# Batch 1's attention earlier and its x transposed by DMA, with the loads of batches 2 and 3 held until those transposes have landed

## The chip, the cores and the metric

The kernel runs on one core of a Trainium2 chip. The metric is device time in microseconds (us), the median of several executions. The span of a profile (from the first to the last instruction) is about 2 us shorter than the time of the same run. A run is called slow when it lies over 1.5% above the fastest run of the same kernel; such runs are left out of the ratios, but not out of the medians quoted. In the profile's lines PE is TensorE (PEld its loading of weights), ACT ScalarE, DVE VectorE, POOL GpSimd and SPq the queue of SyncE. PSUM is the memory into which TensorE's products go; a PSUM pair is two of its buffers.

## The reference

Linear attention on 8 batches of 8 heads, 576 rows and 64 columns, then two matrix products with a SiLU between them on the 4608 x 512 result.

```python
phi = lambda x: np.where(x > 0, x, np.exp(x) - 1.0) + 1.0
q_p, k_p = phi(q), phi(k)
kv  = np.einsum('bhsd,bhse->bhde', k_p, v)
z   = np.sum(k_p, axis=2)
num = np.einsum('bhsd,bhde->bhse', q_p, kv)
den = np.einsum('bhsd,bhd->bhs', q_p, z)[..., None] + 1e-06
x = (num / den).transpose(0, 2, 1, 3).reshape(4608, 512)
h = x @ w_in                                  # 512 -> 2048
g = h * (1.0 / (1.0 + np.exp(-beta * h)))
out = g @ w_out                               # 2048 -> 512
```

## The kernel before

The kernel is a pipeline over batches. While TensorE computes batch b's first product (H, four x tiles of 128 rows against w_in) and its second (Y, against w_out), the attention of batch b+1 is put between the matmuls, from a `plan` that says after which group of matmuls what is issued. In the text, H2 is the first product of batch 2 and Y1 the second product of batch 1. A batch has four x tiles of 128 rows and a tail of 64; two batches' tails are done together at the end.

The scheduling that the change touches, cut:

```python
load_w_out(2); load_v(1); load_w_out(3)        # the queue of loads during H0
...
load_next(2)                                   # k, q, v of batch 2
h_last(0, xT[0], [])
...                                            # batch 1: exponentials, relu, phi, v copy
y_phase_wide(0, {
    4: [F(load_next, 3)],                      # k, q, v of batch 3
    10: [F(q_trans, 1, 0, 1, 2, 3), F(kv_mm, 1), F(kv_evac, 1), F(w_out_scale, 3, 2)],
    11: [F(num_mm, 1, 0), F(num_norm, 1, 0)],
    12: [F(num_mm, 1, 1), F(num_norm, 1, 1), F(x_trans, 1, 0, wide=True)],
    13: [F(num_mm, 1, 2), F(num_norm, 1, 2), F(x_trans, 1, 1, wide=True)],
    14: [F(num_mm, 1, 3), F(num_norm, 1, 3), F(q_trans, 1, 4)],
})
h_phase(1, ...)                                # x_trans(1, 2), x_trans(1, 3), load_v(4) in it
h_last(1, xT[1], [F(exp_, 2, 0), F(exp_, 2, 1)])   # 16 matmuls, exponentials, 4 SiLUs
exp_(3, 1); exp_(3, 0); silu_table()
y_phase_wide(1, {
    1: [F(phi, 2, 0), F(q_trans_dma, 2), F(phi, 2, 1)],
    6: [F(kv_mm, 2), F(kv_evac, 2)],
    8: [F(num_mm, 2, 0), F(num_norm, 2, 0)],   # 9, 10, 11: tiles 1, 2, 3
    ...
})
```

`kv_mm` is the product of keys and values. `num_mm` multiplies one tile of q_pT, the transposed phi(q), with it; `num_norm` divides on VectorE and gives x, which `x_trans` transposes (into xT) on TensorE or, from batch 2 on, one DMA per tile. `q_trans_dma` transposes all of phi(q) of a batch by one DMA. Loads are issued by GpSimd and cast fp32 to bf16; transposes by DMA and stores are issued by SyncE. A load is held back so: GpSimd first copies one element of the tile that must be there.

```python
def hold(a):
    nc.gpsimd.tensor_copy(held, a)

def held_v(b, n):                              # v of b behind q_pT of n
    if b < B:
        hold(st[n, "qT"][0:1, NJ, KC - 1, 0:1])
        load_v(b)
```

## Time and profile before

| | before |
|---|---|
| time, median of 3 (range) | 292.67 us (292.13 to 292.94) |
| span of the profiled run | 290.1 us |
| TensorE busy | 281.8 us, 97% |
| H1, Y1 start | 51.56, 66.44 us |
| batch 2: key-value product, first product with q_pT | 72.57, 75.06 us |
| H2 starts | 82.04 us |

Positions are us from the start of the span.

The granted clock, one digit for each of 40 equal slices of the span in tenths of full speed (the 7 is at the start-up):

```profile
PEclk9799999999999999999999999999999999999999
```

### The profile page before, as it was taken

What the parts mean: (1) busy time and instruction counts of PE and PEld (TensorE: products, weight loads), DVE (VectorE), ACT (ScalarE), POOL (GpSimd) and SP (SyncE); (2) the same over time, 40 slices, a digit from 0 to 9 for tenths busy, and PEclk for the clock granted to TensorE, in tenths of its full rate; (3) what the DMA queues carried; (4) which work ended last, traced back from release to release, by engine and by line L of the source; (5) the groups of instructions that cost most, each with busy time, mean ns of one, the idle gap of its engine ahead of it and who ended that gap; (6) DMA issues with size and microseconds to landing.
All of it is one profiled execution on the core that took longest, in us unless ns stands there. A gap on an engine that the chain in (4) does not pass through costs nothing.

```text
span 290.1 us, 4739 instructions
## 1 busy us (share of the span) xinstructions
PE 281.8 (97%) x1895; PEld 144.1 (50%) x1895; DVE 116.7 (40%) x235; ACT 174.0 (60%) x232; POOL 54.3 (19%) x79
## 2 busy tenths in 40 slices
PE   8889999999999999999999999999999999999994
PEld 3567445644576444454444444554455444444443
DVE  3784487504670365326532654163517300110021
ACT  2788798889998843875277617771750086018500
POOL 8924564400051205020402040000000000000000
PEclk9799999999999999999999999999999999999999
DMA  8999999999379956977894879433503500120033
GB/s 143 196 206 345 254 281 194 257 167 158 62 208 180 136 140 106 196 103 162 121 211 53 161 92 197 77 103 107 97 2 90 111 36 0 72 76 0 0 74 73
DMA packets 75766, 38.07 MB, mean 131 GB/s; under 512 B 43344, under 2 KB 70240, under 8 KB 75744
## 3 DMA queue, kind: packets, MB, share of 16 engines
q0 software_dynamic: 38912, 20.19, 49.0%
q1 hardware_dynamic: 36640, 17.44, 25.7%
q8 instruction: 15, 0.25, 0.4%
q10 hardware_dynamic: 192, 0.14, 0.2%
q14 instruction: 7, 0.06, 0.1%
HBM read 36.71 MB, written 9.44 MB: 159 GB/s over the span
## 4 chain that ended last, share of the span: by engine, by line
PE 92%; DMA 3%; POOL 3%; ACT 1%; issue 0%; DVE 0%; POOLq 0%
PE mm L527 42%; PE mm L475 41%; PE att L421 3%; DMA w_in<-in_moe_w_in_dram 3%; PE att L475 2%; PE att L362 2%; POOL xqk L135 1%; PE mm L559 1%; POOL vraw L135 1%; ACT q_pT L387 1%; PE mm L455 0%; PE att L395 0%; PE att L455 0%; DVE xT L385 0%; DVE y_sb L385 0%
## 5 line engine op out<-in xcount | busy, mean ns | idle before, releaser
L467 ACT ACTIVATE g<-mm,beta_c 128x512 bf16<-128x512 f32 (+2 forms) x160 | 97.8, 623 | 87.1 <-PE mm L475 87.0
L527 PE MATMUL mm<-w_out,g 128*128 128x512 bf16 x560 | 128.0, 379 | 0.0
L475 PE MATMUL mm<-xT,w_in 128*128 128x512 bf16 (+2 forms) x576 | 107.6, 344 | 1.3 <-DMA w_in<-in_moe_w_in_dram 1.2
L475 PEld LDWEIGHTS <-w_in 128*128 128x128 bf16 x672 | 63.8, 98 | 60.8 <-DMA w_in<-in_moe_w_in_dram 1.3
L527 PEld LDWEIGHTS <-g 128*128 128x128 bf16 x560 | 53.1, 98 | 59.0 <-issue 0.3
L537 DVE COPY y_sb<-mm 128x512 f32<-128x512 f32 x27 | 18.7, 692 | 72.9 <-PE mm L527 69.4
L229 ACT ACTIVATE e<-xqk 128x2560 bf16<-128x2560 bf16 x14 | 31.9, 2328 | 0.1
L242 DVE TENSOR_TENSOR qk_p<-r,e 128x2560 bf16<-128x2560 bf16 x14 | 20.8, 1491 | 12.8 <-ACT e L229 12.1
L437 DVE TENSOR_TENSOR xs<-att,rden 128x512 bf16<-128x512 f32 x36 | 24.9, 691 | 1.2
L372 DVE CAST kv_bd<-att 64x260 bf16<-64x260 f32 x14 | 6.0, 427 | 36.6 <-PE att L362 36.5
L435 DVE TENSOR_SCALAR den<-att 128x8 f32<-128x8 f32 x36 | 5.9, 163 | 26.8 <-PE att L421 26.8
L421 PEld LDWEIGHTS <-q_pT 128*128 128x128 bf16 (+1 forms) x160 | 11.1, 102 | 9.5 <-issue 1.3
L421 PE MATMUL att<-kv_bd,q_pT 128*128 128x130 bf16 (+1 forms) x160 | 14.8, 226 | 0.4 <-ACT q_pT L387 0.3
L475 PE MATMUL mm<-xT_tail,w_in 128*128 128x512 bf16 x64 | 14.0, 379 | 0.0
L595 POOL COPY held<-xT 1x1 bf16<-1x1 bf16 x4 | 2.0, 509 | 63.6 <-DMA xT<-xs 63.6
L237 DVE TENSOR_SCALAR r<-xqk 128x2560 bf16<-128x2560 bf16 x14 | 11.9, 853 | 4.0 <-DMA xqk<-in_q_dram 2.5
L612 PE MATMUL mm<-g 128*128 128x512 bf16 x30 | 9.3, 464 | 1.2 <-DVE g L145 1.2
L229 ACT ACT_TABLE_LOAD x7 | 9.0, 1283 | 0.1
L72 POOL DMA_DIRECT2D vraw<-in_v_dram x7 | 6.4, 909 | 10.1 <-DVE vaug L385 4.2
L72 POOL DMA_DIRECT2D xqk<-in_q_dram x7 | 7.1, 1021 | 3.9 <-ACT w_out L214 2.1
L436 DVE RECIPROCAL rden<-den 128x8 f32<-128x8 f32 x36 | 7.3, 203 | 1.2
L72 POOL DMA_DIRECT2D xqk<-in_k_dram x7 | 6.5, 935 | 5.3 <-DMA w_in<-in_moe_w_in_dram 2.5
(77 smaller groups left out, 138.1 us busy)
## 6 DMA issues: line engine op xcount, KB each, us to landing
out_dram<-y_sb SPq DMA_DIRECT2D x28, 256.0 KB, 2.4
xqk<-in_k_dram POOLq DMA_DIRECT2D x7, 512.0 KB, 9.0
xqk<-in_q_dram POOLq DMA_DIRECT2D x7, 512.0 KB, 10.7
vraw<-in_v_dram POOLq DMA_DIRECT2D x7, 512.0 KB, 12.2
w_in<-in_moe_w_in_dram POOLq DMA_DIRECT2D x4, 512.0 KB, 10.1
g<-in_moe_w_out_dram POOLq DMA_DIRECT2D x4, 512.0 KB, 10.9
out_dram<-y_sb SPq DMA_DIRECT2D x14, 128.0 KB, 5.2
xqk<-in_moe_w_out_dram POOLq DMA_DIRECT2D x2, 512.0 KB, 13.7
```

The costliest lines, as they stand in the source:

```text
L72: eng.dma_start(out=dst[:, :, 0:NJ, :].rearrange("p h j d -> p h (j d)"), in_=src[b, :, 0:MAIN, :].rearrange("h (p j) d -> p h (j d)", j=NJ),)
L229: nc.scalar.activation(st[b, "e", a][:, h0:h1], xqk[b % NX][:, a, h0:h1], ACTF.Exp)
L237: nc.vector.tensor_scalar(st[b, "r", a][:, h0:h1], xqk[b % NX][:, a, h0:h1], 0.0, 1.0, ALU.max, ALU.add)
L242: nc.vector.tensor_tensor(st[b, "p"][:, a].rearrange("p j (h d) -> p h j d", h=H)[:, h0:h1], st[b, "r", a][:, h0:h1], st[b, "e", a][:, h0: ...
L421: nc.tensor.matmul(nps[r0 : r0 + n, p // 2, c0 : c0 + 2 * (D + 1)], st[bb, "qT"][:, t, p, :n], kv_bd[bb % 2][:, p], start=True, stop=True, ...
L436: nc.vector.reciprocal(rden[:n], den[:n])
L437: nc.vector.tensor_mul(xs[:n], nv[:, :, :, 0:D], rden[:n, :, :, None].to_broadcast([n, 2, 4, D]))
L467: nc.scalar.activation(g_sb[b % 2][:, ff, c0:c1], hp[:, c0:c1], ACTF.Silu, scale=beta_c[:, ff : ff + 1],)
L475: nc.tensor.matmul(hp[:, c0:c1], w_in_sb[ff // 4][:, kc, (ff % 4) * P : (ff % 4 + 1) * P], x[:, t0:t1, kc, :] if b < B else x[:, kc, c0:c1 ...
L527: nc.tensor.matmul(yp, g_sb[b % 2][:, ff, t * P : (t + 1) * P], w_out_sb[ff // 4][:, ff % 4, :], start=(ff == 0), stop=(ff == FC - 1),)
L537: nc.vector.tensor_copy(y_sb, yp)
L612: nc.tensor.matmul(st["warm"], g_sb[0][:, FC - 1, 0:P], g_sb[0][:, FC - 1, :], start=True, stop=True, skip_group_check=True,)
```

## The change

The intent: bring batch 1's attention forward by two groups of Y0 (with v of batch 1 loaded earlier for it), so that x is ready early enough to be transposed by DMA, which takes 16 transposes off TensorE; and to keep the queue free for these DMAs, load batches 2 and 3 only behind them.

```diff
-    def by_dma(b):
-        return b >= DMA_T
+    def by_dma(b, t):
+        return b > 0 or t == NJ
...
-    load_w_out(2)
     load_v(1)
+    load_w_out(2)
     load_w_out(3)
...
-    load_next(2)
     h_last(0, xT[0], [])
...
     y_phase_wide(0, {
-        4: [F(load_next, 3)],
-        10: [F(q_trans, 1, 0, 1, 2, 3), F(kv_mm, 1), F(kv_evac, 1), F(w_out_scale, 3, 2)],
-        11: [F(num_mm, 1, 0), F(num_norm, 1, 0)],
-        12: [..., F(x_trans, 1, 0, wide=True)],
-        13: [..., F(x_trans, 1, 1, wide=True)],
+        7: [F(kv_mm, 1), F(w_out_scale, 2, (0, 1), False), F(q_trans, 1, 0, 1, 2, 3),
+            F(kv_evac, 1), F(w_out_scale, 2, (2, 3))],
+        9: [F(num_mm, 1, 0), F(num_norm, 1, 0), F(w_out_scale, 3, range(4), False)],
+        10: ...                                  # num_mm and num_norm of tiles 1, 2, 3
     })
+    def load_late():
+        hold(xT[1][0:1, NJ - 1, KC - 1, 0:1])    # the fourth x tile of batch 1
+        for b in (2, 3):
+            load_k(b)
+            load_q(b)
+            if b == 2:
+                load_v(b)
     h_phase(1, xT[1],
-        [(ff, 0, 2) for ff in range(4)] + [(ff, 2, 4) for ff in range(4)] + ALL[4:12],
+        [(ff, 0, 2) for ff in range(8)] + [(ff, 2, 4) for ff in range(8)] + ALL[8:12],
-            0: [F(x_trans, 1, 2), ...], 1: [F(x_trans, 1, 3)], ... 12: [..., F(load_v, 4)],
+            0: [F(load_late), ...], ...
...
-        6: [F(kv_mm, 2), F(kv_evac, 2)],         # in Y1
+        6: [F(kv_mm, 2), F(kv_evac, 2), F(held_v, 3, 2)],
...
-            plan[7 + o] = [F(v_copy, n), F(held_v, b + 3, n)]
+            plan[7 + o] = [F(v_copy, n), F(held_v, n + 1, n)]
```

v of batch 3 is now held behind q_pT of batch 2 (and each later v one batch later than before). And most of the scaling of w_out's second half moves to ScalarE.

More of the change, by code (lines that the diff above doesn't have):

```diff
@@ L40 @@
     EA = D + 2
-    DMA_T = 2
     TINY = 2.0 ** -30
@@ L205, in make_beta, with w_out_scale @@
         nc.vector.reciprocal(rbeta, beta_c)
-    def w_out_scale(i, on_dve=4):
-        for c in range(4):
+    def w_out_scale(i, cs=range(4), dve=True):
+        for c in cs:
             ff = 4 * i + c
             dst, src, by = w_out_sb[i][:, c, :], w_out_f[i][c // 2][:, c % 2, :], rbeta[:, ff : ff + 1]
-            if c < on_dve:
+            if dve:
                 nc.vector.tensor_scalar(dst, src, by, None, ALU.mult)
@@ L439, in num_norm @@
         )
-        if by_dma(b) or t == NJ:
+        if by_dma(b, t):
             nc.sync.dma_start_transpose(
@@ L583, in y_phase_wide @@
             run(plan, 12 + t)
-    def load_next(b):
-        if b < B:
-            load_k(b)
-            load_q(b)
-            load_v(b)
     held = consts.tile([1, 1], BF16)
@@ L664 @@
     qb2 = att_banks(BF16)
+    load_v(1)
     load_w_out(2)
-    load_v(1)
     load_w_out(3)
@@ L703 @@
     exp_(1, 0)
-    silu_table()
     relu(1, 1)
     relu(1, 0)
-    w_out_scale(2)
     phi(1, 1)
+    v_copy(1)
     phi(1, 0)
-    v_copy(1, 0, HH)
-    v_copy(1, HH, H, dve=False)
     y_phase_wide(0, {
-        4: [F(load_next, 3)],
-        10: [
-            F(q_trans, 1, 0, 1, 2, 3), F(kv_mm, 1), F(kv_evac, 1), F(w_out_scale, 3, 2),
-        ],
-        11: [F(num_mm, 1, 0), F(num_norm, 1, 0)],
-        12: [F(num_mm, 1, 1), F(num_norm, 1, 1), F(x_trans, 1, 0, wide=True)],
-        13: [F(num_mm, 1, 2), F(num_norm, 1, 2), F(x_trans, 1, 1, wide=True)],
-        14: [F(num_mm, 1, 3), F(num_norm, 1, 3), F(q_trans, 1, 4)],
-    })
+        7: [
+            F(kv_mm, 1), F(w_out_scale, 2, (0, 1), False), F(q_trans, 1, 0, 1, 2, 3),
+            F(kv_evac, 1), F(w_out_scale, 2, (2, 3)),
+        ],
+        9: [F(num_mm, 1, 0), F(num_norm, 1, 0), F(w_out_scale, 3, range(4), False)],
+        10: [F(num_mm, 1, 1), F(num_norm, 1, 1)],
+        11: [F(num_mm, 1, 2), F(num_norm, 1, 2), F(silu_table)],
+        12: [F(num_mm, 1, 3), F(num_norm, 1, 3)],
+        13: [F(q_trans, 1, 4)],
+    })
+    def load_late():
[5 more added lines that the diff above has]
+                load_v(b)
     ALL = [(ff, 0, 4) for ff in range(FC)]
@@ L725 @@
         1, xT[1],
-        [(ff, 0, 2) for ff in range(4)] + [(ff, 2, 4) for ff in range(4)] + ALL[4:12],
+        [(ff, 0, 2) for ff in range(8)] + [(ff, 2, 4) for ff in range(8)] + ALL[8:12],
         {
-            0: [F(x_trans, 1, 2), F(num_mm, 1, 4), F(num_norm, 1, 4)],
-            1: [F(x_trans, 1, 3)],
-            8: [F(begin, 2), F(relu, 2, 0)],
-            10: [F(relu, 2, 1)],
-            12: [F(v_copy, 2), F(load_v, 4)],
+            0: [F(load_late), F(num_mm, 1, 4), F(num_norm, 1, 4)],
+            12: [F(begin, 2), F(relu, 2, 0)],
+            14: [F(relu, 2, 1)],
+            16: [F(v_copy, 2)],
         },
```

## The prediction

> **What bounds the kernel now.** I read the page's engine shares first, then the chain that ended last, then that chain between 33 and 84 us, where the change acts.
>
> ```profile
> PE 281.8 (97%) x1895; PEld 144.1 (50%) x1895; DVE 116.7 (40%) x235; ACT 174.0 (60%) x232; POOL 54.3 (19%) x79
> PE 92%; DMA 3%; POOL 3%; ACT 1%; issue 0%; DVE 0%; POOLq 0%
> ```
>
> TensorE is busy 97% and is 92% of the chain. The rest (DMA, POOL) is the start-up before 17 us, which the change leaves alone, and 1% of ACT. So time can come only from TensorE instructions removed or TensorE waits removed, and a new wait costs its full length. From batch 2 on the chain is TensorE alone; the only holes after start-up lie in batch 0's second product (Y0) and the start of batch 1's first product (H1):
>
> ```profile
> 33.53 9.50 PE mm L527 x44
> 43.02 0.91 PE att L395 x16
> 43.95 1.95 ACT q_pT L387 x2
> 47.16 0.38 PE mm L527
> 47.77 0.34 PE att L455 x4
> 49.20 0.22 PE att L455 x4
> 52.16 0.22 PE mm L455 x4
> 53.28 0.22 PE mm L455 x4
> 66.60 6.04 PE mm L527 x28
> 72.64 0.75 PE att L362 x40
> 75.23 0.23 PE att L421 x4
> ```
>
> Columns: start, length, what. The L455 rows are the four groups of batch 1's x transposes: 0.34 + 3 x 0.22 = 1.00 us. The ACT row is the copy of q's transposes out of PSUM; batch 1's key-value product and four Y matmuls run behind it, so it costs only the 0.3 us of idle TensorE that the wait view charges to it. The last three rows are Y1's start, batch 2's key-value product and the first product with q_pT: contiguous, no wait. A full ff-group of four 128x512 matmuls takes 0.863 us (6.04 / 7).
>
> Two more views give the slack for batch 2:
>
> ```profile
> 63.89 1.28 ACT L229 ACT_TABLE_LOAD   x1
> 65.18 4.56 ACT L229 ACTIVATE e<-xqk 128x2560 bf16<-128x2560 bf16 x2
> 71.06 2.42 ACT L467 ACTIVATE g<-att,beta_c 128x512 bf16<-128x512 f32 x4
> 69.11 3.08 SPq L407 DMA_TRANSPOSE q_pT<-qk_p  x1
> 83.97 4.41 SPq L407 DMA_TRANSPOSE q_pT<-qk_p  x1
> DMA to landing us min/median/max: 4.8/4.8/4.8
> DMA to landing us min/median/max: 10.3/10.3/10.3
> 64.00:67.00 3.00, 3.00 (x16) 1.37 (x14) 0.00 (x0) 2.99 (x2) 0.00 (x0) 1.00 1.59 191
> ```
>
> Batch 2's exponentials follow the last H1 SiLU at once, their data long there. Its q_pT transpose by DMA is issued at 69.11 and lands 4.8 us later (first landing line), at 73.95: 1.1 us before its use at 75.06 on the timeline. Batch 3's, issued while two loads ran, took 10.3 us (second line). The last row is a window with only loads of q, k and v in the queue: 191 GB/s of written bytes, so one load (576 x 512 x 2 B = 590 KB) takes 590 / 191 = 3.1 us.
>
> **What the Trainium skill says.** "DMA: Bandwidth & Descriptors", section "Queues, rings and completion order", states that each DMA engine goes round-robin between the queues that have work. The trace agrees: q_pT's 4.8 us becomes 10.3 beside two loads. "TensorE: Matmul & The Clock Gate", Part 4, gives about 275 ns for a 128x128 transpose in a kernel; here four in a row take 0.22 us of the chain, 55 ns each, and the measurement decides. Its Part 1 says that an idle window of about 3.4 us halves the clock; before shows 9 in every clock slice after start-up, with no such gap. "ScalarE: Activation LUTs", "What ACT_TABLE_LOAD costs", gives 1283 ns plus a drain of 1380 ns; the trace has 1.28 and the exponential 0.01 us behind it, so I count 1.28 alone.
>
> **The change part by part.**
>
> *x of batch 1 by DMA.* Removed: 16 TensorE transposes, 1.00 us of the path, with the small gaps around them. H1's content is 64 x 0.216 = 13.8 us plus two transpose groups (0.44) and the tail product (0.35), 14.6 against 14.9 measured from 51.56 to 66.44, so about 0.3 of gaps goes too. Four ACT copies (0.60 each) go, off the path. Added: four DMA transposes, 2.4 us each on an idle queue.
>
> *H1 in 16 half groups instead of 8.* Half matmuls cost 0.109 against 0.108 for half a full one: 16 more pairs, under 0.05 us. Tiles 2 and 3 are wanted only 8 x 0.435 = 3.5 us into H1.
>
> *v1 ahead of w_out's third quarter.* v1 lands some 2.4 us earlier (about 39.7 instead of 42.1), the quarter 3.1 later (42.1 instead of 39.0). Its ACT half needs only its first DMA (about 40.8).
>
> *Attention two groups earlier.* TensorE reaches the spot at 33.4 + 8 x 0.863 = 40.3. k's phi ends about 40.0, v's copy (0.82) 40.9, q's phi (1.49) 42.4. The key-value product waits 0.6 us, q's transposes then 0.7; their copies end at 45.4, and after two Y groups TensorE waits 0.3. Idle in Y0 thus becomes 1.6 us, against 1.0 before (18.2 of window less 17.2 of work). Work falls by the two transpose groups there (0.56). Net zero: H1 starts about where it did, 51.6 to 51.8.
>
> *w_out's fourth quarter on ACT.* Four copies at 0.72 = 2.9 us after 45.4, plus the table load (1.28 + 0.20), so Y0's first output copy ends near 50.3. The fourth x transpose stands behind that tile's two stores in SP's queue: issued near 52.0, landing near 54.4. Wanted at 51.8 + 0.35 + 3.5 = 55.6: no wait.
>
> Subtotal: 0.8 us less in H1 (0.44 transposes, 0.3 gaps), 0 to -0.3 in Y0. Y1 would begin near 66.0 instead of 66.6.
>
> *Batches 2 and 3 behind x.* Here time is given back. The hold waits for the fourth transpose (54.4), the first k issue follows about 1 us later (1.5 and 1.0 in later batches). A first load lands 6.1 to 6.5 us after issue, each next one 3.1 later, plus 0.4 for its tail rows: k2 62, q2 65.2, v2 68.3, k3 71, q3 74.5; Y0's six remaining stores and the tail transpose share the engines in the first of these, say 1 us more on each. Before, all were in by 70.8, with two further v loads.
>
> Consequences, each after the last:
> 1. In the program the exponential's table load waits for q2. q2 at 65.5 instead of before 63: exponentials 66.8 to 71.4, table 72.7, SiLUs 12 and 13 by 73.9. The PSUM pair they free is what batch 2's key-value product needs; TensorE is there at 66.0 + 6.0 = 72.1. Wait 1 to 2 us.
> 2. v2 at 68.7, copy to 69.5, q's phi to 71.0, q_pT issued 71.1 instead of 69.1 (VectorE does the v copy before phi).
> 3. q_pT now runs beside k3's end and q3: 4.8 us plus the 2 to 3 us of loading left, landing 77 to 78.5.
> 4. First use wanted at 72.1 + 0.75 + 1.73 = 74.6 plus wait 1. Whatever wait 1 already took is not paid again; the end is set by q_pT's landing.
>
> So that product starts at 76 (no store contention, hold done by 53.5) to 79, instead of 75.06: +0.9 to +3.9, middle about +2.3, all of it carried to the end, since everything later is TensorE without waits. The gain in Y0 and H1 is contained in this difference: it only enlarges the wait.
>
> **Rivals.**
> - *The gain stands.* If loads or q_pT are quicker than that (by the hold ending near 52, or q_pT getting through ahead of q3 as batch 3's did ahead of q4, landing 94.3 against 97.5), the wait vanishes and 0.6 to 1.3 us is saved: 291.3 to 292.0. For it: the schedule looks tuned by someone who saw this collision, since batch 3's v is now held behind q_pT. Against: five loads at 3.1 us after 54 cannot end before 72.
> - *x lands late.* The fourth transpose slips past 55.6 because stores share the queue, and H1 waits at its ninth half group, up to 1 us, and the loads slip with it: 295 to 297.
> - *Worse than summed.* The waits add up to over 3.4 us in one piece and the clock drops, or Y0's waits for v1 and w_out are longer (w_out's second half after 45): 297 to 298.
> - *Nothing moves:* the gain equals the wait: 292.7. Later batches offer no gain, as their chain has no hole.
>
> **Range and chances.** Mechanism gives +2.3 on 292.67 = 295.0, with a spread of about 1.5. I give the tuned-schedule rival about a quarter (291.5): 0.75 x 295.0 + 0.25 x 291.5 = 294.1; I say 294.2. Eight times in ten between 290.9 and 297.3. Two per cent is 5.9 us: faster needs 286.8, more than all idle TensorE time between 33 and 84 us; slower needs 298.5, a wait longer than any I find. 1% faster, 96% the same, 3% slower.
>
> **What the profile after will show.** Right: no x transposes of batch 1 on TensorE; four DMA transposes near 47, 48.3, 49.6 and 52, landing in about 2.4 us; the hold ending near 54 to 55; a TensorE wait at batch 2's key-value product or its first product with q_pT, 1 to 4 us together, charged to SiLU on ACT and to the q_pT landing; q_pT of batch 2 taking 6 to 8 us instead of 4.8; from H2 on the same lengths as before, shifted. Wrong: contiguous TensorE from 66 to 82, or q_pT landing in under 5.5 us, would show that the late loads are free, and the time would be near 291.5. A hole in H1 would show the second rival; more than 2 us of waits in Y0 would show that moving attention up was too early.

## The result, and the profile after

| | before | after |
|---|---|---|
| time, median (range) | 292.81 us (292.13 to 293.19) | 297.54 us (296.89 to 297.91) |
| span of the profiled run | 290.1 us | 295.7 us |
| Y1 starts | 66.44 | 65.73 |
| batch 2's key-value product | 72.57 | 75.83 |
| first product with q_pT | 75.06 | 79.80 |
| H2 starts | 82.04 | 87.95 |

The kernel before has a fourth run here, so its median is not the 292.67 above. The ratio is 1.0162 (95% interval 1.0135 to 1.0189): slower by 1.6%, within the 2% that count as the same. Here and below a ratio is the mean time of one kernel's fast runs over the mean of the other's of the same rounds, so it is not quite the ratio of the medians quoted. 297.54 lies 0.24 us above the upper end of the predicted range and 3.3 above the point.

The page's clock line and the chain that ended last, after:

```profile
PEclk9799999999799999999999999999999999999998
PE 70%; DMA 15%; issue 9%; POOL 2%; ACT 1%; DVE 1%; ACTq 0%; POOLq 0%
```

Before, the chain was TensorE to 92%. Now 15% of it is DMA: the chain runs through the loads. And there is a second 7 in the clock, in the slice from 74 to 81 us.

TensorE's waits, after (what waited, what ended it, total us, how often, the longest):

```profile
PE att L362 <- ACT g L467: 3.9, 1, 3.9
PE mm L475 <- DMA xT<-xs: 1.0, 1, 1.0
```

Both are new and lie at batch 2's key-value product and at H2's start. Y0 has two waits, 0.36 us for batch 1's v copy and 0.67 for phi of q; the prediction put them at 0.6 and 0.7, and a third, of 0.3, did not come. What else the view lists lies in the start-up, but for 0.33 us of issue in the second fence below.

The timeline around the first wait, before and then after (start, duration, engine, line, what; in brackets how long the engine had been idle and what ended it):

```profile
72.57 0.82 PE L362 MATMUL att<-vaug,qk_p 128*64 128x65 bf16 x40
73.33 1.90 PE L527 MATMUL mm<-w_out,g 128*128 128x512 bf16 x8
...
75.06 0.40 PE L421 MATMUL att<-kv_bd,q_pT 128*128 128x130 bf16 x4
```

```profile
67.35 1.28 ACT L229 ACT_TABLE_LOAD   x1 [4.18 <-DMA xqk<-in_q_dram]
...
72.73 4.16 SPq L407 DMA_TRANSPOSE q_pT<-qk_p  x1
...
75.83 1.31 PE L362 MATMUL att<-vaug,qk_p 128*64 128x65 bf16 x40 [3.90 <-ACT g L467]
77.48 2.49 PE L527 MATMUL mm<-w_out,g 128*128 128x512 bf16 x7 [0.33 <-issue]
79.80 0.40 PE L421 MATMUL att<-kv_bd,q_pT 128*128 128x130 bf16 x4
...
87.95 4.31 PE L475 MATMUL mm<-xT,w_in 128*128 128x256 bf16 x38 [1.01 <-DMA xT<-xs]
```

Read the second fence downwards as one chain. ScalarE stood idle for 4.18 us until q of batch 2 landed at 67.3; its table and the exponentials (68.64 to 73.20) follow; then come another table and, from 74.52, the SiLUs. The PSUM pair that the first two SiLUs free is what the key-value product writes to, so TensorE starts that at 75.83 and not at 71.94. The product then takes 1.31 us instead of 0.82, and the Y matmuls behind it 2.49 us for 7 in the record, against 1.90 for 8. The clock explains that. Windows of the profile after (window, length, busy us and count of each engine, granted clock, DMA share, GB/s):

```profile
72.28:75.69 3.41, 0.00 (x0) 0.11 (x1) 1.88 (x2) 3.38 (x5) 0.00 (x0) 1.00 1.62 195
75.69:79.11 3.42, 2.95 (x44) 1.91 (x45) 0.85 (x2) 3.39 (x5) 0.07 (x1) 0.50 0.94 176
79.11:82.52 3.41, 3.41 (x26) 1.94 (x25) 2.15 (x7) 3.41 (x2) 1.68 (x3) 1.00 0.35 45
```

A window of 3.41 us with no matmul is followed by one at clock 0.50. The transposes by DMA, from issue to landing (least, median, most): first q_pT of batch 2, then H2's four x tiles, both after; before they took 4.8, as shown in the prediction, and 2.4.

```profile
DMA to landing us min/median/max: 6.2/6.2/6.2
DMA to landing us min/median/max: 3.4/4.7/5.8
```

Where the 5.6 us of span went, then, along TensorE (the profiled run of before took 292.05 us, that of after 297.91, the slowest of its four, so this is more than the 4.7 us between the medians):

- The first product with q_pT moved by 79.80 - 75.06 = 4.74 us. q_pT had landed at 78.92 (issued 72.73 plus 6.19), so the data alone set 78.92 - 75.06 = 3.86 of it. The key-value product at 75.83 plus before's 2.49 us from there to the first product with q_pT would have been ready at 78.3, earlier than that. The halved clock made it 79.80: another 0.88.
- From there to H2 it took 8.15 us instead of 6.98: +1.17, of which 1.01 is the wait for H2's x.
- From H2 to the end it took 207.75 instead of 208.06: -0.31.
- Sum: 3.86 + 0.88 + 1.17 - 0.31 = 5.60.

What was gained before Y1, 66.44 - 65.73 = 0.71 us, is contained in the first line: it only made the wait longer. This is the split of one profile. In that of pad_only below, the same program but for an unused buffer, the wait in Y1 was 4.3 us with two windows at half clock behind it, H2 did not wait, and the span was 295.4.

### The profile page after: what moved, and what is told of

Its sections match the earlier page's. It is cut to its first block, busy times and chain, and to the rows that moved or that the text cites. A ratio compares the mean times of both kernels' runs of the same rounds, so it can differ in the third digit from the quotient of the medians.

```text
span 295.7 us, 4738 instructions
## 1 busy us (share of the span) xinstructions
PE 280.5 (95%) x1874; PEld 145.3 (49%) x1895; DVE 114.8 (39%) x231; ACT 174.5 (59%) x235; POOL 53.4 (18%) x82
## 4 chain that ended last, share of the span: by engine, by line
PE 70%; DMA 15%; issue 9%; POOL 2%; ACT 1%; DVE 1%; ACTq 0%; POOLq 0%
PE mm L475 33%; PE mm L527 32%; DMA xqk<-in_k_dram 7%; DMA xqk<-in_q_dram 3%; DMA w_in<-in_moe_w_in_dram 2%; PE att L421 2%; DMA xT<-xs 2%; PE att L362 2%; PE mm L559 1%; ACT e L229 1%; POOL g L110 1%; POOL xqk L134 1%; POOL xqk L71 1%; DVE xs L437 0%; ACT L467 0%
## 5 line engine op out<-in xcount | busy, mean ns | idle before, releaser
L475 PEld LDWEIGHTS <-w_in 128*128 128x128 bf16 x688 | 65.4, 98 | 59.7 <-DMA xT<-xs 1.5
L237 DVE TENSOR_SCALAR r<-xqk 128x2560 bf16<-128x2560 bf16 x14 | 11.4, 822 | 17.6 <-DMA xqk<-in_q_dram 16.1
L589 POOL COPY held<-xT 1x1 bf16<-1x1 bf16 x5 | 1.2, 233 | 66.6 <-DMA xT<-xs 66.6
L589 POOL COPY held<-q_pT 1x1 bf16<-1x1 bf16 x5 | 0.9, 176 | 54.3 <-DMA q_pT<-qk_p 54.3
L362 PE MATMUL att<-vaug,qk_p 128*64 128x65 bf16 x280 | 6.3, 203 | 4.3 <-ACT g L467 3.9
L606 PE MATMUL mm<-g 128*128 128x512 bf16 x29 | 8.5, 444 | 1.3 <-DVE g L144 1.2
L362 PEld LDWEIGHTS <-qk_p 128*64 128x64 bf16 x280 | 5.5, 118 | 7.3 <-DVE qk_p L242 3.3
## 6 DMA issues: line engine op xcount, KB each, us to landing
xqk<-in_q_dram POOLq DMA_DIRECT2D x7, 512.0 KB, 10.7
```

What stands on the lines that cost most here:

```text
L237: nc.vector.tensor_scalar(st[b, "r", a][:, h0:h1], xqk[b % NX][:, a, h0:h1], 0.0, 1.0, ALU.max, ALU.add)
L362: nc.tensor.matmul(kvp[g * D : (g + 1) * D, p, :], st[b, "p"][:, 1, j, c0 : c0 + D], vaug[b % 2][:, j, 2 * p + g, 0 : D + 1], start=(j == ...
L475: nc.tensor.matmul(hp[:, c0:c1], w_in_sb[ff // 4][:, kc, (ff % 4) * P : (ff % 4 + 1) * P], x[:, t0:t1, kc, :] if b < B else x[:, kc, c0:c1 ...
L606: nc.tensor.matmul(st["warm"], g_sb[0][:, FC - 1, 0:P], g_sb[0][:, FC - 1, :], start=True, stop=True, skip_group_check=True,)
```

## The experiments

The theory after reading the two traces: the loss is the late loads, in three instalments (a wait in Y1, the halved clock it brings on, and transposes by DMA that are slow beside loads); x by DMA, behind a quiet queue, and the earlier attention cost nothing. One rival: x by DMA or the earlier attention costs time by itself. Another: the late loads alone would fit, and only with the rest of the change do they hurt. No version below beat the kernel before.

### Which part costs: three parts apart

**late_loads_only**: the kernel before, with nothing but the loads moved.

```diff
# against the kernel before
-    load_next(2)
-        4: [F(load_next, 3)],
-            1: [F(x_trans, 1, 3)],
+            1: [F(x_trans, 1, 3), F(load_late)],
-            12: [F(v_copy, 2), F(load_v, 4)],
+            12: [F(v_copy, 2)],
-        6: [F(kv_mm, 2), F(kv_evac, 2)],
+        6: [F(kv_mm, 2), F(kv_evac, 2), F(held_v, 3, 2)],
-            plan[7 + o] = [F(v_copy, n), F(held_v, b + 3, n)]
+            plan[7 + o] = [F(v_copy, n), F(held_v, n + 1, n)]
```

> The kernel before with one part of the change: the loads of batches 2 and 3 held behind batch 1's last x tile (x by TensorE as before, attention where it was). Theory (the late loads cost the time): q2 lands near 67, the exponentials of batch 2 start near 68.6, TensorE waits over 3 us at batch 2's key-value product, batch 2's q_pT lands near 79, H2 waits about 1 us for x behind v3's load; time 297 to 298.5, 1.5 to 2% above before. Rival (the loss comes from x by DMA and the attention moved up): within 0.5% of before, no wait in Y1.

Measured: 297.48 us against 292.09 of the kernel before in the same rounds, ratio 1.0176 (1.0143 to 1.0209). The second rival falls: the late loads alone bring a loss as large. But not at the place that I had seen after. TensorE's longest wait of this run behind the start-up:

```profile
PE mm L475 <- DMA xT<-xs: 2.1, 1, 2.1
```

q of batch 2 came at 65.4, 1.9 us earlier than after: here all eight stores of Y0 were issued by 54.3, ahead of the first late load at 55.64, where after six of them were issued from 53.14 on, among the loads. q_pT took 6.16 us, so Y1 lost 1 us in all (0.5 at the key-value product, 0.5 at the first product with q_pT). This wait is at H2's start, for x of batch 2, which is transposed by DMA in the kernel before too; now v of batch 3 loads beside it. And the windows there:

```profile
82.84:86.25 3.41, 1.32 (x6) 0.42 (x6) 3.38 (x3) 1.74 (x4) 0.00 (x0) 1.00 1.44 178
86.25:89.66 3.41, 3.40 (x17) 2.35 (x18) 1.00 (x2) 1.42 (x3) 2.13 (x4) 0.50 1.08 338
```

TensorE was busy for 1.32 us of the first window and still got half the clock in the next: H2's first 84 matmuls took 13.11 us instead of 11.47. So a hole of 2.05 us, short of a window, cost 2.05 + 1.6. Another 0.8 us of this profile's span was lost before Y0, where no load had moved yet (H1 began at 52.37, not 51.56).

**loads_as_before**: the changed kernel with the loads where they were before (`load_next(2)`, `load_next(3)` and `load_v(4)` back, `load_late` and the hold of v of batch 3 out).

> The changed kernel with the loads of batches 2 and 3 (and v4) put back where before had them, x of batch 1 still by DMA. Theory: Y1 and H2 lose their waits, but batch 1's x transposes now share the engines with six loads and land 6 to 8 us after issue instead of 2.5, so H1 waits 3 to 6 us at its start and at its ninth half group; time 295 to 298. Rival (the hold was needless): the transposes are in time, 291.5 to 292.3, faster than before by what the x transposes cost on TensorE.

Measured: 297.07 us, ratio 1.0155 (1.0127 to 1.0183). With early loads the kernel is as slow, in another place. Y1 and H2 are clean, but H1 waits at its start, for its first two x tiles (it began at 56.06; the second tile landed at 55.92), and behind this wait comes a window at clock 0.50, from 55.66 to 59.08:

```profile
PE mm L475 <- DMA xT<-xs: 4.5, 1, 4.5
DMA to landing us min/median/max: 7.0/8.0/8.4
```

The second line is batch 1's four transposes, beside the loads of batches 2 and 3. In the changed kernel, where those loads wait, the same four landed in:

```profile
DMA to landing us min/median/max: 2.4/2.5/2.5
```

So the hold was needed for x by DMA. That is the dilemma of the change: with loads in the queue, x comes three times later; with the queue quiet, the loads come too late.

**attention_early_only**: loads as before, x of batch 1 by TensorE, but v of batch 1 first and attention two groups earlier.

```diff
# against loads_as_before
-        return b > 0 or t == NJ
+        return b > 1 or t == NJ
-        12: [F(num_mm, 1, 3), F(num_norm, 1, 3)],
-        13: [F(q_trans, 1, 4)],
+        12: [F(num_mm, 1, 3), F(num_norm, 1, 3), F(x_trans, 1, 0, wide=True, dve=True)],
+        13: [F(q_trans, 1, 4), F(x_trans, 1, 1, wide=True, dve=True)],
+        14: [F(x_trans, 1, 2, wide=True, dve=True)],
-            0: [F(num_mm, 1, 4), ...],          # H1
+            0: [F(x_trans, 1, 3, dve=True), F(num_mm, 1, 4), ...],
```

> v1 ahead of w_out's third quarter and the attention two groups earlier, but x of batch 1 by TensorE and all loads as before. Theory (these two parts are neutral): 292.0 to 293.3, within 0.3% of before, Y0 with 1.0 to 1.6 us of idle TensorE, no wait in Y1. Rival (the early attention costs): Y0 longer by over 1 us, 294 or more.

Measured: 292.38 us, ratio 1.0012 (0.9982 to 1.0042). Neutral, as the prediction had it ("Net zero"): Y0 waits 0.36 and 0.67 us and H1, Y1 and H2 not at all.

The three together: earlier attention +0.1%; with it x by DMA and early loads +1.6%; late loads without x by DMA +1.8%; all together +1.6%. The parts do not add: in the profiles the hold takes away H1's hole and puts holes in Y1 and H2 in its place.

**half_dma**: only the third and fourth x tiles by DMA, wanted later, because H1 runs 12 half groups on the first two tiles.

```diff
# against attention_early_only
-        return b > 1 or t == NJ
+        return b > 1 or t == NJ or (b == 1 and t > 1)
-        14: [F(x_trans, 1, 2, wide=True, dve=True)],
-        [(ff, 0, 2) for ff in range(8)] + [(ff, 2, 4) for ff in range(8)] + ALL[8:12],
+        [(ff, 0, 2) for ff in range(12)] + [(ff, 2, 4) for ff in range(12)],
-            0: [F(x_trans, 1, 3, dve=True), F(num_mm, 1, 4), F(num_norm, 1, 4)],
+            0: [F(num_mm, 1, 4), F(num_norm, 1, 4)],
```

> An attempt at a better version: the run attention_early_only, with only batch 1's x tiles 2 and 3 by DMA and H1's first 12 groups split in halves, so that these tiles are wanted 5.2 us into H1. Theory: the two transposes land 8 us after issue, near 58, just when wanted; 8 TensorE transposes less: 0.3 to 0.6 us under attention_early_only, 291.8 to 292.1, so at best 0.2% under before. Rival (they come too late): a wait of 1 to 2 us in H1, and with it perhaps a half-speed window, 293 to 295.

Measured: 293.15 us, ratio 1.0037 (1.0014 to 1.0061). The two tiles took 7.0 and 7.4 us beside the loads, and H1 still waited 0.88 us, more than the 8 transposes saved; the clock stayed full. A miss as a version, but it shows that the slow transposes cost only what their use cannot wait for.

### Links of the chain

**no_y0_stores**: Y0's stores of tiles 1 to 3 are left out, the rest is the changed kernel. Its output is wrong, which doesn't matter for the time. These stores share the DMA engines with the first late loads.

```diff
             if b == 0:
+                if t > 0:
+                    return
```

> The changed kernel without the stores of Y0's tiles 1 to 3 (a wrong result on purpose: these rows of the output stay unwritten). Theory (the stores in the queue when the hold ends delay the first loads more than I had reckoned): q2's tail lands near 65 instead of 67.3, everything behind it 2 to 2.5 us earlier, the wait at batch 2's key-value product 1.5 to 2 us instead of 3.9, q_pT lands near 76.5: 2.5 to 3.5 us under the changed kernel, about 294.5. Rival (the loads are slow by themselves): q2 lands within 0.5 us of 67.3 and the time stays within 0.5 us.

Measured: 295.61 us, ratio 1.0127 (1.0096 to 1.0157), short of the gain expected: 1.9 us under the changed kernel's 297.54 by the medians, but only 1.0 by the ratios, whose intervals overlap, so the gain in time is not clear of noise. The link itself is. The main part of batch 2's q, from issue to landing, with the stores and then without:

```profile
DMA to landing us min/median/max: 10.7/10.7/10.7
DMA to landing us min/median/max: 8.7/8.7/8.7
```

All of q was there at 65.17 instead of 67.28 (0.3 of this comes from the start-up). In four other profiles below whose loads up to there are the changed kernel's (silu_first, v3_behind_x2, pad_only, after_no_v3) the main part took 10.4 to 11.4 us, so 8.7 is outside that scatter. The stores were worth about 2 us to it, with what stood behind them: the transpose of batch 1's tail, next in SyncE's queue, now landed at 55.65, before the loads, instead of 66.66, among them. The wait for the key-value product was 2.1 us and not 3.9, but it was still followed by half the clock:

```profile
71.59:75.00 3.41, 1.30 (x44) 1.10 (x44) 1.44 (x2) 3.38 (x6) 0.00 (x0) 1.00 1.46 166
75.00:78.41 3.41, 3.41 (x13) 1.48 (x12) 0.74 (x4) 3.40 (x3) 1.03 (x2) 0.50 0.46 104
```

The first window was busy for 1.30 us, and still the next is at 0.50: that part of the loss stayed.

**silu_first**: in the changed kernel, ScalarE does H1's last SiLUs ahead of batch 2's exponentials, so the PSUM pair comes free early.

```diff
-    h_last(1, xT[1], [F(exp_, 2, 0), F(exp_, 2, 1)])
+    h_last(1, xT[1], [])
+    exp_(2, 0)
+    exp_(2, 1)
```

> The changed kernel with H1's last four SiLUs ahead of batch 2's exponentials on ACT instead of behind them, so that the PSUM banks of the key-value product come free before Y1 starts. Theory: a second chain stands only 1 us behind the one removed (q2, exponentials, phi of k, done at 74.7), so the product starts near 74.8 instead of 75.8, and q_pT's landing near 78.9 stays: 0.5 to 1.0 us off. Rival (the PSUM banks are the cause): the wait of 3.9 us goes altogether, 3 us or more off.

Measured: 296.96 us, ratio 1.0187 (1.0144 to 1.023) with one run at 300.09; not to be told from the changed kernel. The wait at the key-value product moved to another releaser:

```profile
PE att L362 <- DVE qk_p L242: 2.8, 1, 2.8
```

VectorE's phi of k, which needs the exponential, which needs q and k. So SiLU on ScalarE was only the last of two chains, both hanging on the late q, the second about 1 us behind. The half clock stayed, and H2's wait in this profile was 1.7 us.

**v3_behind_x2**: v of batch 3 is loaded only when batch 2's x tiles have landed.

```diff
             hold(xT[n % 3][0:1, NJ - 1, KC - 1, 0:1])      # in held_kq
+            if n == 2:
+                load_v(3)
-        6: [F(kv_mm, 2), F(kv_evac, 2), F(held_v, 3, 2)],
+        6: [F(kv_mm, 2), F(kv_evac, 2)],
```

> The changed kernel with v3's load held behind batch 2's last x tile instead of behind batch 2's q_pT. Theory: batch 2's x transposes land in 2.5 us again (they took 3.4 to 5.8 beside v3), the hole of 1.0 us of TensorE at the start of H2 goes, the waits in Y1 stay; 0.8 to 1.5 us under the changed kernel, 296.1 to 296.8. Rival (the hole in H2 is only a shadow of the waits in Y1, or v3 then comes too late for its copy): no change, or slower.

Measured: 298.88 us, ratio 1.0227 (1.0184 to 1.027), not under the changed kernel. H2's hole is gone: x of batch 2 landed in 2.4 to 2.5 us. So that load was what slowed these transposes. But v of batch 3, whose main part took 9.3 us, was then complete at 99.1, and batch 3's key-value product waited for its copy: 1.8 us (the other 0.4 is Y0's). In Y1 the 3.6 us and the half clock stayed.

```profile
PE att L362 <- DVE vaug L385: 2.2, 2, 1.8
97.11:100.53 3.42, 1.62 (x34) 0.77 (x34) 0.83 (x1) 1.54 (x3) 1.12 (x3) 1.00 1.53 184
100.53:103.94 3.41, 3.36 (x38) 1.71 (x33) 0.85 (x2) 1.68 (x3) 0.67 (x1) 1.00 1.63 188
```

The windows are of use for the clock: 1.62 us busy out of 3.42, so 1.80 idle, and the next window stays at full clock.

**zero_fill**, **zero_fill_kv** and **pad_only**: to measure the clock's part by itself, fill the wait in the changed kernel with 16 matmuls whose weights are zero, adding into Y1's sums.

```diff
+    zeros = consts.tile([P, P], BF16)           # and a memset; pad_only is these two alone
+    def zero_fill(n):
+        for _ in range(n):
+            nc.tensor.matmul(st["yp"][0], zeros, w_out_sb[0][:, 0, :], start=False, stop=False)
-        6: [F(kv_mm, 2), F(kv_evac, 2), F(held_v, 3, 2)],
+        6: [F(zero_fill, 16), F(kv_mm, 2), F(kv_evac, 2), F(held_v, 3, 2)],
```

zero_fill_kv takes its zeros from a block of kv_bd that is always zero, in place of a new buffer, with 17 matmuls.

> The changed kernel with 16 matmuls of zero weights added into Y1's first accumulation, which change nothing in it, placed where TensorE waits 3.9 us for batch 2's key-value product, so that it is busy in that time. Theory: the key-value product still starts near 75.8 (ACT's SiLU frees its PSUM then), the clock record shows no half-speed window of 3.4 us after it, the key-value product takes 0.75 instead of 1.31 us and the Y groups after it 0.86 instead of about 1.5, and the first product with q_pT then stands on q_pT's landing near 78.9 instead of 79.8: 0.5 to 1.0 us off, about 296.7. Rival 1 (the clock alone carries the loss): 1.6 us off or more. Rival 2 (the half-speed window has nothing to do with the wait): it is still there, nothing gained.

Measured: 301.12 us, ratio 1.0317 (1.0283 to 1.0351), a miss. The fill ran from 71.53 to 75.36, but k and q of batch 2 came 1.6 to 3.7 us later than in the changed kernel, before the fill had begun (q at 69.06), so the key-value product began at 77.62. 2.26 us of idle TensorE were left and brought on half the clock, and at H2 2.06 us brought it on again. Was it where the new buffer pushed the others?

> The changed kernel with zero_fill's unused 256-byte buffer and its memset, and no fill. If the place of the buffers slows the loads: near 300, q2 near 69. If not: 297.5, q2 near 67.3, and the fill was the cause.

> The zero-weight fill again, with no new buffer: 17 matmuls with a 64x64 block of zeros that the kernel holds anyway, in the changed kernel's wait. In zero_fill the first loads after the hold landed 1.8 to 2.4 us later than in the changed kernel, before any fill ran, which I cannot explain; a new 256-byte buffer had moved every later one. Theory (that move was the cause, and the clock costs 0.5 to 1.0 us on the path): loads as in the changed kernel (q2 near 67.3), no half-speed window near 76, 296.5 to 297.0. Rival (the fill itself slows the kernel): 300 or more again.

Measured: pad_only 297.15 us, ratio 1.0162, just the changed kernel. zero_fill_kv had one run of 374.33 us, at clock 0.756, whose cause is open; its three fast runs lay at 299.16 to 302.21, ratio 1.0308 (1.0265 to 1.0351). So neither buffer nor placement is it. Why a fill that starts later goes with later loads is left open (part may be scatter: after_no_v3's q came at 68.21 with no fill), and the clock's part was not measured by itself in this way.

### Attempts to mend it

**mended**: k of batch 2, for which there is a free buffer, is loaded ahead of the hold; v of batch 3 is held behind batch 2's second x tile; the products with q_pT move one group back.

```diff
+    load_k(2)
     h_last(0, xT[0], [])
...                                              # load_late: k of batch 3 only
-        6: [F(kv_mm, 2), F(kv_evac, 2), F(held_v, 3, 2)],
-        8: [F(num_mm, 2, 0), F(num_norm, 2, 0)], # to 11
+        6: [F(kv_mm, 2), F(kv_evac, 2)],
+        9: [F(num_mm, 2, 0), F(num_norm, 2, 0)], # to 12
+        10: [F(num_mm, 2, 1), F(num_norm, 2, 1), F(v3_late)],
```

> An attempt at a version that beats both: the changed kernel with k2 loaded ahead of the hold (it fills the idle queue before the x transposes), v3 held behind batch 2's second x tile, and batch 2's numerators one Y1 group later. Theory: q2 lands near 63, no wait at the key-value product, q_pT lands near 75.5 and is wanted at 75.2, H2 starts near 81.5 without a hole: 291.5 to 292.7. Rival (the stores and transposes around 55 delay the loads as before): q2 near 65, a wait of about 1 us, 293 to 294.

Measured: 299.86 us over all six runs, ratio 1.0235 (1.0202 to 1.0269) without two slow ones near 302. The profiled run was the fastest, 297.19. The wait in Y1 is gone in its profile (q of batch 2 at 62.95, q_pT at 75.57). But batch 2's fourth x tile took 7.3 us beside v of batch 3 and Y1's stores, and H2 waited 3.76 us, with half the clock after it.

**mended2**: as mended, but v of batch 3 held as in the changed kernel, and each store of `y_phase_wide` issued behind that group's plan, so that the fourth x transpose stands ahead of the stores.

```diff
-            y_out(b, t, yp[t], on_act=True)
+            y_sb = work.tile([P, DM], F32, tag="y_sb", name="y_sb", bufs=4)
+            nc.scalar.activation(y_sb, yp[t], ACTF.Copy)
             run(plan, 12 + t)
+            store(b, t, y_sb)
```

> A second attempt. The profile of the first showed no wait at batch 2's key-value product (q2 landed at 63.0) and no half-speed window in Y1, but a wait of 3.8 us in H2 for batch 2's fourth x tile, which landed 7.3 us after issue beside v3. Here v3 is held behind batch 2's q_pT again, as in the changed kernel, and Y0's first stores stand behind batch 1's fourth x transpose in SP's queue, so that the hold ends 1.4 us earlier. Theory (the loss is the sum of the waits that late loads make, and nothing else in the change costs): q2 near 61.6, q_pT of batch 2 near 74.5, v3 near 81.5, x tiles of batch 2 near 81 to 84, H2 starting near 81.5 with a wait under 0.5 us: 291.5 to 292.7, the same as before or 0.2% under it, with no half-speed window after start-up. Rival (v3 still collides with the x transposes): a wait of 1 to 2 us at the start of H2, 293 to 294.5.

Measured: 297.44 us (295.89 to 299.36), ratio 1.0187 (1.0145 to 1.0228). Y1 again has no wait; H2's x took 4.7 to 7.1 us beside the load of v of batch 3, H2 waited 3.2 us, and the clock was halved for two windows, 84.32 to 91.15.

**mended2_no_v3** and **after_no_v3**: v of batch 3 is not loaded at all (the `F(held_v, 3, 2)` is left out), in mended2 and in the changed kernel. Their outputs are wrong, which doesn't matter for the times. If that load is the last thing in the way, mended2 without it should be at the time of the kernel before or under it.

> The second attempt without v3's load (a wrong result on purpose: batch 3 computes with batch 1's v). Theory (what is left of the loss there is v3 beside batch 2's x transposes, and the half-speed windows after the wait it makes): the transposes land in 2.5 us, H2 starts near 82.2 with no wait, no half-speed window after start-up, 291.5 to 292.7. Rival (some further cost of the change): 294 or more.

> The changed kernel without v3's load (the same wrong result on purpose). Theory: the wait in H2 goes (1.0 to 1.3 us), the wait of 3.9 us in Y1 and its half-speed window stay: 296.0 to 296.8. Rival (v3 is the cause of the whole loss): 293 or less.

Measured: mended2_no_v3 294.26 us, with runs from 291.5 to 296.37 (the last slow), ratio 1.0054 (0.9988 to 1.0119) from three fast runs that lie 1.4% apart; after_no_v3 297.33, ratio 1.0202 (1.0145 to 1.0259). So in mended2 that load costs 1.3% by the ratios; in the changed kernel its absence makes no difference in time: H2's hole is gone, but in that profile q came 0.9 us later and the wait in Y1 was 4.8 us instead of 3.9. The profile of mended2_no_v3, one of its faster runs (292.84), has no half clock, though TensorE waited 2.3 us for q_pT, which took 7.7 us beside the other loads:

```profile
72.46:75.87 3.41, 2.07 (x10) 0.75 (x8) 0.28 (x1) 3.40 (x3) 0.00 (x0) 1.00 0.72 159
75.87:79.29 3.42, 2.43 (x20) 1.49 (x21) 1.85 (x6) 3.40 (x2) 0.00 (x0) 1.00 0.00 0
79.29:82.70 3.41, 3.41 (x21) 1.71 (x20) 3.17 (x9) 1.78 (x5) 0.00 (x0) 1.00 0.51 102
```

The wait of 2.3 us, longer than the 2.1 that halved the clock elsewhere, fell across two windows: 1.34 and 0.99 idle.

**mended3**: mended2 with v of batch 3 loaded right behind v of batch 2, without a hold, and the products with q_pT one further group back.

```diff
             if b == 2:
-                load_v(b)
+                load_v(2)
+                load_v(3)
```

> A third attempt at a version that beats both, with a right result: v3 loaded straight behind v2, with no hold, ahead of k3 and q3, and batch 2's numerators one Y1 group later again. Theory: k3 and q3 land 3 us later (q3 near 76.7), in time for batch 3's exponentials; q_pT of batch 2 shares the engines longer and lands near 78, wanted at 76.8: a wait of about 1.2 us, short enough for the clock; x tiles of batch 2 in time: 292.5 to 293.5, so not better than before. Rival: q_pT in time, 291.5 to 292.

Measured: 297.91 us, ratio 1.0212 (1.0185 to 1.0239). Now q_pT runs beside three loads and takes 11.2 us, from 69.28 to 80.43; TensorE waits 4.5 us for it and the clock is halved from 80.6.

```profile
PE att L421 <- DMA q_pT<-qk_p: 4.5, 1, 4.5
```

Wherever the five or six late loads were put, they met a transpose by DMA that TensorE was waiting for: q_pT, or batch 2's x. In the kernel before, where x of batch 1 needs no DMA, they run during Y0, H1 and the first 1.2 us of Y1: q of batch 3 has landed at 64.6 us, v of batch 3 at 67.6.

## Why the prediction was wrong

The direction and the mechanism held: the late loads give back more than x by DMA brings, through q of batch 2, q_pT's landing and the first product with q_pT. The size did not: +2.3 us was the middle, the time rose by 4.7 (the profiled spans by 5.6).

- *H1, Y0 and x by DMA*: right. H1 started at 51.38 (51.6 to 51.8 predicted), the x transposes were issued at 46.5, 47.9, 49.2 and 51.8 and landed in 2.4 to 2.5 us, H1 had no hole, Y1 began at 65.73 ("near 66.0"; the prediction took its 66.6 for before from the chain, where the timeline has 66.44, so its positions in Y1 are some 0.2 us late). Attention moved earlier was neutral, as its experiment shows.
- *The loads (step 1)*: the start was right (hold done at 54.29, first issue at 54.77). The share of the queue was mis-sized: I named "say 1 us more" for Y0's stores and the tail's transpose, and carried only 0.3 of it on, to q at 65.5. It landed at 67.28; its main part took 10.7 us from issue, and 8.7 without these in the way: the term is about 2 us. With it, the wait at the key-value product was 3.9 us and not "1 to 2".
- *q_pT (steps 2 and 3)*: issued at 72.73 instead of 71.1, 1.6 us late by the same term: v of batch 2, loaded behind q, landed at 70.35 instead of 68.7, and its copy stands ahead of phi. q_pT took 6.19 us, under the "4.8 us plus 2 to 3" (which add to a landing at 77.9 to 78.9, not to the 77 to 78.5 that I wrote). q_pT landed at 78.92, at the upper end of that sum.
- *Step 4, the sum*: "the end is set by q_pT's landing". That is the step that failed. The landing itself is worth 3.86 us, the upper end of "+0.9 to +3.9" and not its middle: 1.6 us of mis-sized term. Two terms were not in the sum (their sizes are those of one profile). Half the clock put the product 0.88 us behind that landing. I had that only among the rivals, as "Worse than summed", with a condition of over 3.4 us in one piece and a time of 297 to 298. That rival came true: the wait was 3.9 us, the clock halved, the time 297.54. Its condition was too strict: late_loads_only and no_y0_stores show that 2.05 to 2.1 us can do. Finally, "everything later is TensorE without waits" is wrong: H2's x tiles are transposed by DMA beside the load of v of batch 3, which the change had put there; they took up to 5.8 us and H2 came another 1.17 later. v3_behind_x2 shows the cause: with that load held back they took 2.4 to 2.5. In time, though, neither that run nor after_no_v3, both without the hole in H2, was faster than the changed kernel.
- *2.3 + 1.6 + 0.9 + 1.2 - 0.3 = 5.7*, against 5.6 in the spans.
- *The rivals*: "The gain stands" falls: q_pT took 6.19 us, beyond the 5.5 that I had named for it (and mended2_no_v3, with Y1's wait for q gone and one load fewer, only comes to the time of before). "x lands late" was not so after, but loads_as_before shows it is what the hold prevents. I had not seen that the two are a dilemma: the quarter that I gave to a tuned schedule took 0.8 us off the 295.0 of the mechanism, to 294.2.

What stays open: why the zero matmuls went with later loads, the one execution at clock 0.756, and how the cost splits between the wait in Y1, the clock and H2 in the timed runs, as only one run of each kernel has a profile.

## What to carry to other kernels

Before loads are moved behind something, list every transfer that TensorE will wait for from then on, and count for each what else is in the queue at that time: a transpose by DMA of 2.4 us on a quiet queue was one of 7 to 8 beside loads here. Carry the whole of a contention term through the sum, and follow the loads that the change moves past the first stage that they touch, to every later one. When a new wait on TensorE comes to 2 us or more, reckon with a window at half clock behind it (here 0.9 to 1.6 us more); it did not always come (2.3 us without it in mended2_no_v3).

## What the Trainium skill lacked or had wrong

- "TensorE: Matmul & The Clock Gate", Part 1, puts the throttle at an idle window of about 3.4 us, on a free-running grid. The traces agree with such a grid, of 3.41 us, but a window that is not wholly idle does it too. Behind the start-up, 2.09 us idle of one window (late_loads_only), 2.06 and 2.26 (zero_fill) and 2.11 (no_y0_stores) were each followed by clock 0.50; 1.80 (v3_behind_x2), 1.70 (silu_first) and 1.34 then 0.99 in two windows (mended2_no_v3) were not. This gives no threshold: in the start-up 1.22 us (before, from 8.09) was followed by clock 0.50 and 1.71 (no_y0_stores, from 13.56) was not, and a window already at half clock was followed by another after 1.02 (mended2, from 84.32) and 1.46 (pad_only, from 74.41). What beside idle time decides was not tested.
- "DMA: Bandwidth & Descriptors", "Queues, rings and completion order", has the round-robin between queues but no measure of what it does to a transpose by DMA: a 128 x 512 tile went from 2.4 us to 7.0 to 8.4 beside loads (loads_as_before) and q_pT from 4.8 to 6.2 (after) and 11.2 (mended3).
- No page that I looked at says what a run of stores costs loads queued beside them: here, with the one transpose behind them, about 2 us on the load of q, 10.7 against 8.7 us (no_y0_stores).
